# h of an agent-attention and SoLU kernel in 64-row tiles: three passes over both column halves, p turned two tiles at a time, its parts copied to both row halves by transfers

## The chip, the cores and the metric

The kernel runs on one core of one Trainium2 chip. A time is device microseconds (us) of one execution on that core; several executions give a median. One further execution was profiled, and every row below comes from that one.

## What is computed

Four batches of 12608 rows of q, k and v with 128 columns, and 49 agents per batch. The attention goes through the agents, and its result is the input x of a feed-forward block (50432 rows, 128 to 1024 and back), whose activation is a softmax-weighted h with a layer norm:

```python
a2k = sm(agents, k); agent_v = a2k @ v          # sm: softmax of scale * (a @ b.T)
q2a = sm(q, agents); x = q2a @ agent_v
h = x @ w_in
e = exp(h - max(h)); solu = h * e / sum(e)
ln = (solu - mean(solu)) / sqrt(var(solu) + 1e-06) * g_ln
out = ln @ w_out
```

All of it is float32.

## The kernel before, in words

The rows are handled in 396 tiles of 128 (99 a batch). For each batch, phase A (`phase_a`) makes agent_v in 13 chunks of k and v and multiplies it by w_in, so that h of a row is p times a matrix M with 49 rows and 1024 columns, where p is the row's softmax over the 49 agents. M is held as a high part `mh` and a low part `ml` (float32r, a float32 format that TensorE takes in one pass where float32 takes two), each written twice, into rows 0 to 63 and rows 64 to 127.

Phase B (`phase_b`, units of 8 tiles, each of two groups of four) makes p: `b0` the logits on TensorE (L647), `b1` to `b3r` the softmax, `b4` on GpSimd scales p (L676), rounds it to a high part (L678) and takes the rest as low part (L680), both into one 128-column row of `pack` (49 used columns from 0, 49 from 64), `b5` turns the four tiles on TensorE (L687), `b6` copies them out on ScalarE into `pT` (L692). A column of `pT` so has the high part of p in rows 0 to 63 and the low part in rows 64 to 127.

The rest goes tile by tile (x): `c_h` (L730) makes h in PSUM, for each half of 512 columns one matmul with `mh` and one with `ml`, all 128 rows deep, so that two passes give all four products of parts. Then the row maximum (DVE, L734), exp (ScalarE, L744), u = h*e (DVE, L749), the sum of squares (ScalarE, L755), eight transposes of u (`c_t`, L762), and the split of the turned u into parts: a half that is in `DIR` is split straight from PSUM (ScalarE L777, DVE L786), another is copied to SBUF (ScalarE, L781) and split by GpSimd (L790, L794). `c_w` (L810) multiplies by w_out, 24 matmuls of 256 columns for two tiles. GpSimd's small operations and a transfer through DRAM give the norm's factor (`rB`), and DVE's L875 applies it.

The order of the instructions on each engine is fixed ahead by `Plan`: each operation has an engine, a cost, a due time and those it depends on; the planner simulates the engines and takes among the startable ones the one with the earliest due time. The costs (such as 0.468 for one half of `c_h`) and the due offsets (the table of numbers `BD0` to `AEND`) are constants of the source. `kind` tells it the shape that a matmul uses the array in, and `SWITCH` what a change between kinds costs. An engine never leaves this order, and SyncE issues all transfers from one queue in the planned order too.

Of the kernel before, what the change touches and what calls it, by code (L numbers as in the profile page):

```python
# [9 lines left out]
F32 = mybir.dt.float32  # L10
F32R = mybir.dt.float32r
# [3 lines left out]
ALU = mybir.AluOpType  # L15
# [10 lines left out]
class Plan:  # L26
# [15 lines left out]
    def op(self, eng, fn, cost, due, deps=(), take=False, free=None, after=(), kind=1, shy=0.0):  # L42
        o = Op()
        o.kind, o.shy = kind, shy
        o.eng, o.fn, o.cost, o.due, o.take, o.free = eng, fn, cost, due, take, free
        o.deps, o.outs, o.end, o.bank = [d for d in deps if d is not None], [], None, None
        o.left = 0
        for d in o.deps + [d for d in after if d is not None]:
            if d.end is None:
                o.left += 1  # L50
                d.outs.append(o)
        if not o.left:
            self.push(o)
        return o
# [71 lines left out]
def kernel(  # L126
# [32 lines left out]
    BD0 = 13.69
    BD1 = 15.3  # L160
    BD2 = 9.96
    BD3 = -17.37
    BD4 = 0.17
    BD5 = 5.85
    DH = -3.24
    DMX = -8.66
    DEX = 0.61
    DU_ = -1.62
    DSQ = 20.92
    DT = -0.42  # L170
    DEV = -8.39
    DLD = 1.53
    DSP = -1.16
    DW = 3.3
    DR = 1.58
    DF_ = 5.14
# [12 lines left out]
    DMXL = 15.46  # L189
    DEXR = 5.1  # L190
    DEXL = -1.93
    DUR = -10.64
    DUL = -12.84
    DSQR = -10.36
    DSQL = -12.17
    DTR = -6.53
    DTL = -23.81
    DEVR = -0.65
    DEVL = 9.51
    DLDR = -16.59  # L200
    DLDL = 26.96
    DSPR = -6.09
    DSPL = 14.43
    DWR = 2.46
    DWL = -0.21
    RBL = 6.0
    ASTART = -3.67
    AEND = -2.04
    engs = (mybir.EngineType.PE, mybir.EngineType.Activation, mybir.EngineType.DVE, mybir.EngineType.Pool)
    SCALE = 1.0 / math.sqrt(C)  # L210
    INV = 1.0 / DF
# [422 lines left out]
    def phase_b(k, dues, gate=()):  # L634

        b, t0, nt = units_b[k]
        r = {}
        nq = (nt + GT - 1) // GT

        def b0(j0, j1, px=None):  # L640
            if px is not None:
                r["px"] = px
            qt, px = qts[k], r["px"]
            for j in range(j0, j1):
                for h in range(0, P, AP2):
                    o = col0(t0 + j) - col0(t0) + h
                    nc.tensor.matmul(px[h : h + AP2, j * A : (j + 1) * A], qt[:, o : o + AP2], ag_sb[:, b, :A],  # L647
                                     start=True, stop=True)
            r["lg"] = px[:, : nt * A].rearrange("p (t a) -> p t a", a=A)

        def b1():
            r["mx"] = tiny.tile([P, UB], F32, tag="mx", name=f"mx{b}_{t0}")
            nc.vector.tensor_reduce(out=r["mx"][:, :nt], in_=r["lg"], op=ALU.max, axis=AX.X)

        def b1s():
            mx, lg = r.pop("mx"), r.pop("lg")
            r["e"] = logits[k % 2][:, :nt, :]
            r["d"] = r["e"][:, :, :A]
            nc.vector.tensor_tensor(out=r["d"], in0=lg, in1=mx[:, :nt].unsqueeze(2).to_broadcast([P, nt, A]),
                                    op=ALU.subtract)  # L660

        def b2():
            nc.scalar.activation(out=r["d"], in_=r["d"], func=AF.Exp, scale=SCALE)

        def b3():
            r["s"] = tiny.tile([P, UB], F32, tag="sm", name=f"sm{b}_{t0}")[:, :nt]
            nc.vector.tensor_reduce(out=r["s"], in_=r["e"], op=ALU.add, axis=AX.X)

        def b3r():
            nc.vector.reciprocal(out=r["s"], in_=r["s"])  # L670

        def b4(q):
            m = min(GT, nt - q * GT)
            sl = slice(q * GT, q * GT + m)
            pk, dv = packs[q], r["d"][:, sl, :]
            nc.gpsimd.tensor_tensor(out=dv, in0=dv, in1=r["s"][:, sl].unsqueeze(2).to_broadcast([P, m, A]),  # L676
                                    op=ALU.mult)
            nc.gpsimd.tensor_scalar(out=pk[:, :m, :A].bitcast(F32R), in0=dv, scalar1=1.0, scalar2=0.0,  # L678
                                    op0=ALU.mult, op1=ALU.add)
            nc.gpsimd.tensor_tensor(out=pk[:, :m, AP2 : AP2 + A].bitcast(F32R), in0=dv, in1=pk[:, :m, :A],  # L680
                                    op=ALU.subtract)

        def b5(q, px):
            m = min(GT, nt - q * GT)
            r["pt", q] = px
            for j in range(m):
                nc.tensor.transpose(px[:, j * P : (j + 1) * P], packs[q][:, j, :], ident)  # L687

        def b6(q):
            m = min(GT, nt - q * GT)  # L690
            pT = pTs[b, t0 // GT + q] = bpool.tile([P, GT * P], F32R, tag="pT", bufs=PTB, name=f"pT{b}_{t0}_{q}")
            nc.scalar.copy(out=pT[:, : m * P], in_=r.pop(("pt", q))[:, : m * P])  # L692
# [12 lines left out]
        d2 = op("D", b1s, 0.05 + 0.0532 * nt, dues[1] + 0.1, [d1] + [B4.get((k - 2, q)) for q in range(2)], free=first, shy=shy)  # L705
        a1 = op("A", b2, 0.098 + 0.0402 * nt, dues[2], [d2])
        d3 = op("D", b3, 0.05 + 0.0532 * nt, dues[3], [a1], shy=shy)
        d5 = op("D", b3r, 0.12, dues[3] + 0.2, [d3])
        for q in range(nq):
            g = len(groups)  # L710
            groups.append((b, t0 // GT + q))
            sc = min(GT, nt - q * GT) / GT
            old = B5.get((k - 1, q)) or B5.get((k - 2, q))
            B4[k, q] = op("G", lambda q=q: b4(q), 0.07 + 1.5 * sc, dues[4] + 2.5 * q, [d5, old])
            B5[k, q] = op("P", lambda px, q=q: b5(q, px), 0.435 * sc, dues[5] + 2.5 * q,
                          [B4[k, q], grp_h.get(groups[g - PTB]) if g >= PTB else None], take=True, shy=shy)
            pT_op[groups[g]] = op("A", lambda q=q: b6(q), 0.48 * sc, dues[5] + 2.5 * q + 0.3, [B5[k, q]], free=B5[k, q], shy=shy)
# [5 lines left out]
    def c_h(x, hf):  # L723
        b, t = seq[x]
        g, j = divmod(t, GT)
        ph = phs[x] = ph2[x % 2]
        lhs = pTs[b, g][:, j * P : (j + 1) * P]
        sl = slice(hf * HW, (hf + 1) * HW)
        for m in range(2):
            nc.tensor.matmul(ph[:, sl], lhs, bmats[b]["mh" if m == 0 else "ml"][:, sl], start=(m == 0), stop=(m == 1))  # L730

    def c_max(x):
        nms[x] = tiny.tile([P, 1], F32, tag="nm", name=f"nm{x}")
# [159 lines left out]
    def F(f, *x):  # L893
        return lambda *y: f(*x, *y)
# [30 lines left out]
    def at(x, d, r, l):  # L925
        return x + d + (r * (1.0 - x / 12.0) if x < 12 else l if x >= (B - 1) * TB else 0.0)
# [4 lines left out]
    for x in range(n):  # L931
# [3 lines left out]
        if t % UB == 0:  # L935
# [7 lines left out]
        grp_h[b, t // GT] = last_h[b] = H[x, 1]  # L943
        MX[x] = op("D", F(c_max, x), 1.13, at(x, DMX, DMXR, DMXL), [H[x, 0], H[x, 1]])
# [116 lines left out]
```

## Time and profile before

| | |
|---|---|
| median of 3 executions | 1573.31 us (1573.09 to 1574.97) |
| the profiled execution | 1575.81 us, of which its span 1574.0 us |
| TensorE (PE) busy | 1550.8 us, 99% |
| ScalarE (ACT) busy | 1440.1 us, 91% |
| VectorE (DVE) busy | 1376.5 us, 87% |
| GpSimd (POOL) busy | 1254.5 us, 80% |
| granted TensorE clock, mean | 0.999 |

The span is from the first to the last instruction of the program. Busy is the time in which an engine has at least one instruction running. Matmuls overlap each other in the rows (one of 512 columns is shown with 0.39 us, and the next starts 0.23 us later), so what a matmul costs is read from one start to the next.

### The profile page before, as it was taken

To read this page: it belongs to the slowest core of one execution; us is meant where nothing else is said; L and a number is where in the kernel's file an instruction comes from. 1 tells how busy PE (TensorE), PEld (TensorE's weight loads), DVE (VectorE), ACT (ScalarE), POOL (GpSimd) and SP (SyncE) were. 2 spreads that over 40 slices of the span, in tenths; PEclk is the share of its full clock that TensorE was granted. 3 is DMA by queue.
4 is the path that set the end of the run, shared out by engine and by line. 5 is a ranking of instruction groups with operands and counts; after the bars stand their busy time and mean duration, and the time that the engine had idled before them with its cause. 6 is when DMAs were issued, how large, how long until landed. Compare 5 with 4: busy or idle time off the path is not lost.

```text
span 1574.0 us, 35069 instructions
## 1 busy us (share of the span) xinstructions
PE 1550.8 (99%) x12821; PEld 1381.7 (88%) x12821; DVE 1376.5 (87%) x2161; ACT 1440.1 (91%) x2740; POOL 1254.5 (80%) x1715
## 2 busy tenths in 40 slices
PE   8899999999999999999999999999999999999998
PEld 5588898998889899898899899898988989999998
DVE  6989898888998888889898888988888998989986
ACT  3599999999999999999999998999989999999996
POOL 2577888888788788787888878887878889988896
PEclk9999999999999999999999999999999999999999
DMA  9422323313123223222222232222111121111111
GB/s 370 150 88 81 96 81 95 95 59 103 62 82 100 82 88 105 91 81 74 88 68 88 88 102 88 88 88 87 49 63 53 47 69 55 62 55 49 45 42 40
DMA packets 57629, 133.65 MB, mean 85 GB/s; under 512 B 9840, under 2 KB 14064, under 8 KB 57456
## 3 DMA queue, kind: packets, MB, share of 16 engines
q1 hardware_dynamic: 57456, 131.41, 26.2%
q8 instruction: 101, 1.65, 0.4%
q14 instruction: 72, 0.59, 0.1%
HBM read 105.36 MB, written 26.02 MB: 83 GB/s over the span
## 4 chain that ended last, share of the span: by engine, by line
PE 89%; DVE 4%; ACT 3%; POOL 2%; issue 1%; DMA 0%; SPq 0%; DVEq 0%; ACTq 0%; POOLq 0%
PE px L810 33%; PE ph L730 22%; PE px L762 21%; PE px L647 3%; PE px L467 3%; PE px L418 3%; PE px L687 3%; PE px L451 1%; ACT e L744 1%; DVE u L749 1%; ACT sq L755 1%; DVE nm L734 1%; POOL uL L794 0%; ACT uT L781 0%; DVE mxp L423 0%
## 5 line engine op out<-in xcount | busy, mean ns | idle before, releaser
L794 POOL TENSOR_TENSOR uL<-uT,uH 128x1024 fp32r<-128x1024 f32 (+1 forms) x295 | 598.6, 2029 | 24.3
L734 DVE TENSOR_REDUCE nm<-ph 128x1 f32<-128x1024 f32 x396 | 480.3, 1219 | 55.3 <-PE ph L730 53.3
L749 DVE SCALAR_TENSOR_TENSOR u<-ph,e 128x1024 f32<-128x1024 f32 x396 | 481.0, 1219 | 54.2 <-ACT e L744 30.3
L755 ACT ACTIVATE sq<-u,su 128x1024 bf16<-128x1024 f32 x396 | 464.0, 1172 | 25.9 <-DVE u L749 22.8
L744 ACT ACTIVATE e<-ph,nm 128x1024 f32<-128x1024 f32 x396 | 446.3, 1132 | 28.4 <-DVE nm L734 25.0
L810 PE MATMUL px<-uL,wH 128*128 128x256 f32 x1584 | 467.2, 295 | 0.1
L810 PE MATMUL px<-uH,wH 128*128 128x256 f32 x1584 | 453.5, 286 | 2.6 <-DVE uL L786 1.4
L810 PE MATMUL px<-uH,wL 128*128 128x256 f32 x1584 | 449.4, 284 | 0.0
L762 PE MATMUL px<-ident,u 128*128 128x128 f32 x3168 | 429.4, 274 | 2.6 <-DVE u L749 0.7
L762 PEld LDWEIGHTS px<-ident,u 128*128 128x128 f32 x3168 | 355.6, 141 | 51.5 <-issue 18.7
L790 POOL TENSOR_SCALAR uH<-uT 128x1024 fp32r<-128x1024 f32 (+1 forms) x295 | 268.3, 909 | 85.7 <-ACT uT L781 84.6
L730 PE MATMUL ph<-mh,pT 128*128 128x512 f32 x792 | 326.3, 412 | 0.7 <-DVE u L749 0.4
L810 PEld LDWEIGHTS px<-uH,wH 128*128 128x128 f32 x1584 | 299.7, 189 | 15.4 <-issue 3.8
L730 PE MATMUL ph<-ml,pT 128*128 128x512 f32 x792 | 312.4, 394 | 0.0
L810 PEld LDWEIGHTS px<-uH,wL 128*128 128x128 f32 x1584 | 300.2, 189 | 9.6
L810 PEld LDWEIGHTS px<-uL,wH 128*128 128x128 f32 x1584 | 299.8, 189 | 9.0 <-issue 4.6
L781 ACT COPY uT<-px 128x512 f32<-128x512 f32 x492 | 272.9, 594 | 13.7 <-issue 3.0
L786 DVE TENSOR_TENSOR uL<-px,uH 128x512 fp32r<-128x512 f32 x300 | 200.9, 681 | 28.0 <-ACT uH L777 27.7
L777 ACT CAST uH<-px 128x512 fp32r<-128x512 f32 x300 | 170.1, 603 | 2.9 <-PE px L762 2.6
L730 PEld LDWEIGHTS ph<-mh,pT 128*128 128x128 f32 x792 | 149.2, 188 | 22.6 <-DVE u L749 4.6
L730 PEld LDWEIGHTS ph<-ml,pT 128*128 128x128 f32 x792 | 149.7, 189 | 17.1 <-DVE ml L543 0.2
L829 POOL TENSOR_TENSOR y<-x,nhalf 128x4 f32<-128x4 f32 x99 | 100.1, 1011 | 7.5
(119 smaller groups left out, 1469.2 us busy)
## 6 DMA issues: line engine op xcount, KB each, us to landing
rB<-dr SPq DMA_DIRECT2D x98, 256.0 KB
qt<-in_qT_dram SPq DMA_DIRECT2D x48, 512.0 KB
out_dram<-ob SPq DMA_DIRECT2D x95, 256.0 KB
kt<-in_kT_dram SPq DMA_DIRECT2D x36, 512.0 KB
vt<-in_v_dram SPq DMA_DIRECT2D x36, 512.0 KB
dr<-yr SPq DMA_DIRECT2D x392, 0.5 KB
kh<-in_kT_dram SPq DMA_DIRECT2D x12, 512.0 KB
vh<-in_v_dram SPq DMA_DIRECT2D x12, 512.0 KB
```

What stands on the lines that cost most here:

```text
L730: nc.tensor.matmul(ph[:, sl], lhs, bmats[b]["mh" if m == 0 else "ml"][:, sl], start=(m == 0), stop=(m == 1))
L734: nc.vector.tensor_reduce(out=nms[x], in_=phs[x], op=ALU.max, axis=AX.X, negate=True)
L744: nc.scalar.activation(out=es[x], in_=phs[x], func=AF.Exp, bias=nms.pop(x), accum_out=st[G]["S"][:, j : j + 1])
L749: nc.vector.scalar_tensor_tensor(out=u, in0=phs[x], scalar=INV, in1=es[x], op0=ALU.mult, op1=ALU.mult, accum_out=su)
L755: nc.scalar.activation(out=sq, in_=u, func=AF.Square, bias=su, scale=-float(DF), accum_out=st[G]["Q"][:, j : j + 1])
L762: nc.tensor.transpose(pt[:, kf * P : (kf + 1) * P], us[x][0][:, k0 * P : (k0 + 1) * P], ident)
L777: nc.scalar.copy(out=uH, in_=pt)
L781: nc.scalar.copy(out=rr[x][:, hf * 4 : hf * 4 + 4, :], in_=pt)
L786: nc.vector.tensor_tensor(out=uL, in0=pt, in1=uH.bitcast(F32), op=ALU.subtract)
L790: nc.gpsimd.tensor_scalar(out=uH, in0=rr[x][:, k0:k1, :], scalar1=1.0, scalar2=0.0, op0=ALU.mult, op1=ALU.add)
L794: nc.gpsimd.tensor_tensor(out=uL, in0=rr[x][:, k0:k1, :], in1=uH.bitcast(F32), op=ALU.subtract)
L810: nc.tensor.matmul(po, wt[:, kf, :], ut[:, kf, :], start=(q == 0), stop=(q == WM - 1))
```

## The change

`b4` only scales p now, into a `pack` of 64 columns a tile. `b5` turns two tiles with one transpose: rows 0 to 63 of the result belong to the even tile, rows 64 to 127 to the odd one. `b6` writes the high part from PSUM (half the columns of before), a new `b7` on DVE takes the low part from PSUM and the high part, and a new `b8` issues two transfers from SyncE for each group, which copy rows 0 to 63 to rows 64 to 127 of a second copy and the other way round. `c_h` makes both halves of 512 columns in one operation: six matmuls that are 64 rows deep, the left half in rows 0 to 63 of the array, the right half in rows 64 to 127, in three passes (high with `mh`, high with `ml`, low with `mh`; the product of the low parts is left out). The planner gets the cost 0.82 for all of `c_h` and kind 1 in place of 0. `DIR` is looked up by x % 8: five of sixteen halves go straight, where it was six. The due offsets are other numbers, and `pT` has 6 buffers of twice the size in place of 8.

```diff
-    DIR = {(1, 0), (1, 1), (3, 1)}
+    DIR = {(1, 0), (1, 1), (3, 1), (5, 1), (7, 1)}
...
-    BD4 = 0.17
-    BD5 = 5.85
+    BD4 = 8.39
+    BD5 = 8.87
...
-    PTB = 8
+    PTB = 6
...
-        pk = const.tile([P, GT, P], F32, name=f"pack{i}")
+        pk = const.tile([P, GT, AP2], F32, name=f"pack{i}")
...
-            nc.gpsimd.tensor_scalar(out=pk[:, :m, :A].bitcast(F32R), in0=dv, scalar1=1.0, scalar2=0.0,
-                                    op0=ALU.mult, op1=ALU.add)
-            nc.gpsimd.tensor_tensor(out=pk[:, :m, AP2 : AP2 + A].bitcast(F32R), in0=dv, in1=pk[:, :m, :A],
-                                    op=ALU.subtract)
+            nc.gpsimd.tensor_tensor(out=packs[q][:, :m, :A], in0=r["d"][:, sl, :],
+                                    in1=r["s"][:, sl].unsqueeze(2).to_broadcast([P, m, A]), op=ALU.mult)
...
-            for j in range(m):
-                nc.tensor.transpose(px[:, j * P : (j + 1) * P], packs[q][:, j, :], ident)
+            for j in range(0, m, 2):
+                nc.tensor.transpose(px[:, j * AP2 : (j + 2) * AP2], packs[q][:, j : j + 2, :].rearrange("p j a -> p (j a)"),
+                                    ident)
...
+            nc.scalar.copy(out=pT[:, 0, 0, :w], in_=r["pt", q][:, :w])
+
+        def b7(q):
...
+            nc.vector.tensor_tensor(out=pT[:, 0, 1, :w], in0=r.pop(("pt", q))[:, :w], in1=pT[:, 0, 0, :w].bitcast(F32),
+                                    op=ALU.subtract)
+
+        def b8(q):
...
+            for i in range(2):
+                r0, r1 = i * AP2, (1 - i) * AP2
+                nc.sync.dma_start(out=pT[r1 : r1 + AP2, 1, :, :w].bitcast(F32), in_=pT[r0 : r0 + AP2, 0, :, :w].bitcast(F32))
...
-        for m in range(2):
-            nc.tensor.matmul(ph[:, sl], lhs, bmats[b]["mh" if m == 0 else "ml"][:, sl], start=(m == 0), stop=(m == 1))
+        for q, (part, mm) in enumerate(((0, mh), (0, ml), (1, mh))):
+            for hf in range(2):
+                sl, rows = slice(hf * HW, (hf + 1) * HW), slice(hf * AP2, (hf + 1) * AP2)
+                nc.tensor.matmul(ph[:, sl], pTs[b, g][rows, (hf + j) % 2, part, tok], mm[rows, sl], start=(q == 0), stop=(q == 2))
...
-        for hf in range(2):
-            H[x, hf] = op("P", F(c_h, x, hf), 0.468, at(x, DH, DHR, DHL) + 0.02 * hf,
-                          [pT_op[b, t // GT], U.get(x - 2)] + mdone[b][: hf + 1], kind=0)
+        H[x] = op("P", F(c_h, x), 0.82, at(x, DH, DHR, DHL), [pT_op[b, t // GT], U.get(x - 2)] + mdone[b], kind=1)
```

Three places of the instruction order show what is moved.

PE in the second batch, before: transposes of u (L762), then h of one tile (L730, h in `ph`, p in `pT`) and c_w (L810) right behind it.

```order
L762 MATMUL px_127<-ident,u_9468 128x128 x4
L762 MATMUL px_125<-ident,u_9468 128x128 x4
L810 MATMUL px_124<-uL_9277,wH 128x256
L810 MATMUL px_124<-uH_9276,wL 128x256
L810 MATMUL px_124<-uH_9276,wH 128x256
L810 MATMUL px_124<-uL_9277,wH 128x256
L730 MATMUL ph_122<-mh_5775,pT_64_0_9358 128x512
L730 MATMUL ph_122<-ml_5776,pT_64_0_9358 128x512
L730 MATMUL ph_122<-mh_5775,pT_64_0_9358 128x512
L730 MATMUL ph_122<-ml_5776,pT_64_0_9358 128x512
L810 MATMUL px_124<-uH_9276,wL 128x256
```

PE in the second batch of the change: h is L743 now, transposes of u are L775, c_w is L823, and L467 is phase A's product with v, in tiles of 64 columns.

```order
L823 MATMUL px_126<-uH_9497,wL 128x256
L823 MATMUL px_126<-uH_9497,wH 128x256
L823 MATMUL px_126<-uL_9498,wH 128x256
L467 MATMUL px_124<-vt_9_9080,eT_9_9745 64x128 x8
L743 MATMUL ph_123<-mh_5727,pT_64_0_9520 128x512 x2
L743 MATMUL ph_123<-ml_5728,pT_64_0_9520 128x512 x2
L743 MATMUL ph_123<-mh_5727,pT_64_0_9520 128x512 x2
L775 MATMUL px_125<-ident,u_9715 128x128 x4
L823 MATMUL px_126<-uH_9497,wL 128x256
```

Six matmuls stand where four stood, in pairs on one part of M, and here a tile of phase A is directly ahead of them.

SP's queue in the third batch of the change: L701 are the new transfers, L864 and L865 send the norm's factor, L904 an output, L396 and L407 load k and v.

```order
L864 DMA dr_11971<-yr_11961 4x32 x4
L865 DMA rB_11972<-dr_11971 128x512
L701 DMA pT_8_0_12008<-pT_8_0_12008 64x512 x2
L396 DMA kt_2_12093<-in_kT_dram 128x1024
L904 DMA out_dram<-ob_12108 128x512
L396 DMA kt_3_12131<-in_kT_dram 128x1024
L407 DMA vt_2_12196<-in_v_dram 128x1024
L864 DMA dr_12209<-yr_12204 4x32 x4
L701 DMA pT_8_1_12222<-pT_8_1_12222 64x512 x2
```

Two transfers a group stand between those that were there before, and none of the others is gone.

## Rows read from the trace of the kernel before

**Rows 1.** The page, busy time: engine busy us (share of the span) xinstructions.

```profile
PE 1550.8 (99%) x12821; PEld 1381.7 (88%) x12821; DVE 1376.5 (87%) x2161; ACT 1440.1 (91%) x2740; POOL 1254.5 (80%) x1715
```

**Rows 2.** Windows: stretch, us, busy of PE PEld DVE ACT POOL (instructions), granted clock, DMA.

```profile
0.00:100.00 100.00, 85.24 (x726) 58.69 (x727) 79.14 (x153) 53.49 (x118) 46.04 (x68) 0.98 0.62 223
200.00:600.00 400.00, 398.92 (x3330) 357.34 (x3329) 353.21 (x554) 373.65 (x711) 322.03 (x442) 1.00 0.28 86
1200.00:1500.00 300.00, 298.31 (x2476) 276.64 (x2475) 273.24 (x410) 294.59 (x548) 261.87 (x363) 1.00 0.17 55
```

**Rows 3.** Timeline of PE, one c_h: start us, us, engine, line, out<-in, rows*columns, count.

```profile
810.03 0.40 PE L730 MATMUL ph<-mh,pT 128*128 128x512 f32 x1
...
810.95 0.28 PE L810 MATMUL px<-uH,wL 128*128 128x256 f32 x1
```

**Rows 4.** Timeline of PE around the logits of one unit (L647) and two sets of transposes.

```profile
816.08 0.28 PE L810 MATMUL px<-uH,wL 128*128 128x256 f32 x1
816.19 0.28 PE L810 MATMUL px<-uH,wH 128*128 128x256 f32 x1
816.40 1.14 PE L647 MATMUL px<-ag_sb,qt 128*64 128x49 f32 x32
817.47 0.66 PE L687 MATMUL px<-ident,pack 128*128 128x128 f32 x4
817.96 0.60 PE L762 MATMUL px<-ident,u 128*128 128x128 f32 x4
818.32 0.37 PE L810 MATMUL px<-uL,wH 128*128 128x256 f32 x1
818.52 0.28 PE L810 MATMUL px<-uH,wL 128*128 128x256 f32 x1
```

**Rows 5.** Lines by shape, PE, 480 to 760 us: xcount | busy us, mean ns | idle.

```profile
L810 PE MATMUL px<-uL,wH 128*128 128x256 f32 x290 | 87.2, 301 | 0.0
...
L730 PE MATMUL ph<-mh,pT 128*128 128x512 f32 x144 | 58.0, 403 | 0.0
```

**Rows 6.** Timeline of PE, one chunk of phase A (L418): two tiles of 64 columns.

```profile
219.84 1.08 PE L418 MATMUL px<-kt,ag_sb 128*64 128x512 f32 x4
220.85 1.09 PE L762 MATMUL px<-ident,u 128*128 128x128 f32 x8
```

**Rows 7.** Timeline of PE, one float32 matmul of 512 columns on the full array (L531).

```profile
807.82 1.02 PE L531 MATMUL px<-win_sb,av_dup 128*128 128x512 f32 x2
808.68 0.49 PE L762 MATMUL px<-ident,u 128*128 128x128 f32 x3
```

**Rows 8.** Timeline of PE around a matmul one row deep (L491).

```profile
401.10 0.28 PE L810 MATMUL px<-uH,wL 128*128 128x256 f32 x1
401.31 0.38 PE L491 MATMUL px<-ones,row 1*128 1x1 f32 x2
401.62 0.38 PE L810 MATMUL px<-uH,wH 128*128 128x256 f32 x1
401.84 0.29 PE L810 MATMUL px<-uL,wH 128*128 128x256 f32 x1
```

**Rows 9.** Timelines of PE in narrow windows: L467 turning to a tile 64 rows deep.

```profile
397.06 0.27 PE L467 MATMUL px<-vt,eT 128*64 128x128 f32 x1
...
397.26 0.32 PE L467 MATMUL px<-vt,eT 64*64 64x128 f32 x1
```

**Rows 10.** Timeline of PE, one whole L467 of phase A: 16 matmuls in eight pairs.

```profile
235.70 1.06 PE L467 MATMUL px<-vt,eT 128*64 128x128 f32 x16
236.69 0.44 PE L762 MATMUL px<-ident,u 128*128 128x128 f32 x2
```

**Rows 11.** Lines by shape, ACT: the copy of the turned p.

```profile
L692 ACT CAST pT<-px 128x512 fp32r<-128x512 f32 x96 | 57.7, 601 | 6.0 <-PE px L687 5.8
```

**Rows 12.** Waits of SP's queue: line, waited for, us in total, times, longest us.

```profile
SPq L891 <- DVE ob L875: 459.5, 83, 13.2
...
SPq L852 <- DMA dr<-yr: 53.3, 91, 2.6
```

More of the change, by code (lines that the diff above doesn't have):

```diff
@@ L157 @@
     WC = 4
[L159 to L162, printed above, removed]
-    BD4 = 0.17
-    BD5 = 5.85
[L165 to L176, printed above, removed]
+    BD0 = 11.79
+    BD1 = 12.29
+    BD2 = 10.71
+    BD3 = -17.5
+    BD4 = 8.39
+    BD5 = 8.87
+    DH = -6.46
+    DMX = 0.4
+    DEX = 5.54
+    DU_ = -2.31
+    DSQ = 29.74
+    DT = 0.31
+    DEV = -3.94
+    DLD = 3.07
+    DSP = -17.22
+    DW = 4.65
+    DR = 0.16
+    DF_ = 4.4
     OUTD = -5.86
@@ L188 @@
     DMXR = 10.02
[L189 to L192, printed above, removed]
+    DMXL = 10.71
+    DEXR = -5.26
+    DEXL = -3.36
+    DUR = -9.16
     DUL = -12.84
-    DSQR = -10.36
+    DSQR = -10.39
     DSQL = -12.17
[L196 to L199, printed above, removed]
+    DTR = -6.2
+    DTL = -20.21
+    DEVR = -8.06
+    DEVL = 9.39
     DLDR = -16.59
-    DLDL = 26.96
+    DLDL = 6.55
     DSPR = -6.09
-    DSPL = 14.43
-    DWR = 2.46
+    DSPL = 16.8
+    DWR = 2.63
     DWL = -0.21
     RBL = 6.0
-    ASTART = -3.67
-    AEND = -2.04
+    ASTART = -4.07
+    AEND = 1.37
     engs = (mybir.EngineType.PE, mybir.EngineType.Activation, mybir.EngineType.DVE, mybir.EngineType.Pool)
@@ L685, in b5 @@
             r["pt", q] = px
-            for j in range(m):
-                nc.tensor.transpose(px[:, j * P : (j + 1) * P], packs[q][:, j, :], ident)
+            for j in range(0, m, 2):
+                nc.tensor.transpose(px[:, j * AP2 : (j + 2) * AP2], packs[q][:, j : j + 2, :].rearrange("p j a -> p (j a)"),
+                                    ident)
         def b6(q):
-            m = min(GT, nt - q * GT)
-            pT = pTs[b, t0 // GT + q] = bpool.tile([P, GT * P], F32R, tag="pT", bufs=PTB, name=f"pT{b}_{t0}_{q}")
-            nc.scalar.copy(out=pT[:, : m * P], in_=r.pop(("pt", q))[:, : m * P])
+            w = (min(GT, nt - q * GT) + 1) // 2 * P
+            pT = pTs[b, t0 // GT + q] = bpool.tile([P, 2, 2, GT // 2 * P], F32R, tag="pT", bufs=PTB, name=f"pT{b}_{t0}_{q}")
+            nc.scalar.copy(out=pT[:, 0, 0, :w], in_=r["pt", q][:, :w])
+        def b7(q):
+            w = (min(GT, nt - q * GT) + 1) // 2 * P
+            pT = pTs[b, t0 // GT + q]
+            nc.vector.tensor_tensor(out=pT[:, 0, 1, :w], in0=r.pop(("pt", q))[:, :w], in1=pT[:, 0, 0, :w].bitcast(F32),
+                                    op=ALU.subtract)
+        def b8(q):
+            w = (min(GT, nt - q * GT) + 1) // 2 * P
+            pT = pTs[b, t0 // GT + q]
+            for i in range(2):
+                r0, r1 = i * AP2, (1 - i) * AP2
+                nc.sync.dma_start(out=pT[r1 : r1 + AP2, 1, :, :w].bitcast(F32), in_=pT[r0 : r0 + AP2, 0, :, :w].bitcast(F32))
         shy = SHY if k < 4 else 0.0
@@ L713, in phase_b @@
             old = B5.get((k - 1, q)) or B5.get((k - 2, q))
-            B4[k, q] = op("G", lambda q=q: b4(q), 0.07 + 1.5 * sc, dues[4] + 2.5 * q, [d5, old])
-            B5[k, q] = op("P", lambda px, q=q: b5(q, px), 0.435 * sc, dues[5] + 2.5 * q,
+            B4[k, q] = op("G", lambda q=q: b4(q), 0.08 + 0.53 * sc, dues[4] + 2.5 * q, [d5, old])
+            B5[k, q] = op("P", lambda px, q=q: b5(q, px), 0.218, dues[5] + 2.5 * q,
                           [B4[k, q], grp_h.get(groups[g - PTB]) if g >= PTB else None], take=True, shy=shy)
-            pT_op[groups[g]] = op("A", lambda q=q: b6(q), 0.48 * sc, dues[5] + 2.5 * q + 0.3, [B5[k, q]], free=B5[k, q], shy=shy)
+            a6 = op("A", lambda q=q: b6(q), 0.25, dues[5] + 2.5 * q + 0.3, [B5[k, q]], shy=shy)
+            d7 = op("D", lambda q=q: b7(q), 0.33, dues[5] + 2.5 * q + 0.6, [a6], free=B5[k, q], shy=shy)
+            pT_op[groups[g]] = op("S", lambda q=q: b8(q), (0.12, 0.13 if k else 0, 2.5), dues[5] + 2.5 * q + 0.6, [d7], shy=shy)
         if k + 2 < nu and k + 2 > 1:
@@ L721, with c_h @@
     us, phs, nms, es, rr, pr, st = {}, {}, {}, {}, {}, {}, {}
-    def c_h(x, hf):
+    def c_h(x):
         b, t = seq[x]
@@ L726, in c_h @@
         ph = phs[x] = ph2[x % 2]
-        lhs = pTs[b, g][:, j * P : (j + 1) * P]
-        sl = slice(hf * HW, (hf + 1) * HW)
-        for m in range(2):
-            nc.tensor.matmul(ph[:, sl], lhs, bmats[b]["mh" if m == 0 else "ml"][:, sl], start=(m == 0), stop=(m == 1))
+        mh, ml = (bmats[b][m] for m in ("mh", "ml"))
+        tok = slice(j // 2 * P, j // 2 * P + P)
+        for q, (part, mm) in enumerate(((0, mh), (0, ml), (1, mh))):
+            for hf in range(2):
+                sl, rows = slice(hf * HW, (hf + 1) * HW), slice(hf * AP2, (hf + 1) * AP2)
+                nc.tensor.matmul(ph[:, sl], pTs[b, g][rows, (hf + j) % 2, part, tok], mm[rows, sl], start=(q == 0), stop=(q == 2))
     def c_max(x):
@@ L764, in direct @@
     def direct(x, hf):
-        return (x % GT, hf) in DIR or x >= n - TD
+        return (x % (2 * GT), hf) in DIR or x >= n - TD
     def parts(x, k0, k1):
@@ L939 @@
             ku += 1
-        for hf in range(2):
-            H[x, hf] = op("P", F(c_h, x, hf), 0.468, at(x, DH, DHR, DHL) + 0.02 * hf,
-                          [pT_op[b, t // GT], U.get(x - 2)] + mdone[b][: hf + 1], kind=0)
-        grp_h[b, t // GT] = last_h[b] = H[x, 1]
-        MX[x] = op("D", F(c_max, x), 1.13, at(x, DMX, DMXR, DMXL), [H[x, 0], H[x, 1]])
+        H[x] = op("P", F(c_h, x), 0.82, at(x, DH, DHR, DHL), [pT_op[b, t // GT], U.get(x - 2)] + mdone[b], kind=1)
+        grp_h[b, t // GT] = last_h[b] = H[x]
+        MX[x] = op("D", F(c_max, x), 1.13, at(x, DMX, DMXR, DMXL), [H[x]])
         EX[x] = op("A", F(c_exp, x), 1.11, at(x, DEX, DEXR, DEXL), [MX[x], U.get(x - 2), RB.get(G - 3)] + (cout if x < 2 else []))
```

3 lines of the change are left out of this document (removed).

## The prediction

> **What bounds the kernel now.** First the busy times [rows 1]: PE has 99% of the span, ACT 91%, DVE 87%, POOL 80%. A busy PE need not be a full PE, since a matmul's row lasts longer than its place in the stream, so the windows come next [rows 2]. From 200 to 600 us PE is busy in 398.9 of 400 us and ACT in 373.7. From 1200 to 1500 us, where phase A is over, PE has 298.3 and ACT 294.6 of 300 us: there ACT is close behind. In the first 100 us PE waits for loads and is busy in 85 us.
>
> Then I test whether those PE rows are work or waiting, by giving each matmul the distance from its start to the next start. A pass of h takes 0.23 us, since four take 0.92 [rows 3]. A c_w matmul takes 0.11 to 0.12, four transposes 0.36, and the c_w matmul behind them lasts 0.20 in place of 0.12, so a transpose takes (0.36 + 0.08) / 4 = 0.11 [rows 4]. From 480 to 760 us there are 869 c_w matmuls (290 of one kind [rows 5]), 288 passes of h (144 of one kind [rows 5]), 695 transposes, and 30 runs of narrow matmuls at 1.1 to 1.2 us: 101 + 66 + 76 + 35 = 278 of 280 us. PE hardly waits. The time of the kernel is the sum of what PE is given, and a microsecond more or less on PE is one on the span, until ACT takes over.
>
> **The price that decides: a change of the array's shape.** All big matmuls of before use the full array, 128 rows by 128 columns. Phase A and the logits use tiles of 64 columns, two side by side. Reader, look at the two borders of such a run. Ahead of L647 the last c_w matmul lasts 0.21 us (816.19 to 816.40) where the one before it lasted 0.11: 0.10 us in which nothing streams [rows 4]. L418 has four matmuls of 512 columns in 1.01 us [rows 6], and one such product, two matmuls on the full array, takes 0.86 [rows 7]. So the two tiles do run side by side (else it were 1.72), and 0.15 us are left for leaving the shape and for the first load of weights. The row depth counts as well as the width: going to a matmul one row deep costs 0.21 - 0.12 = 0.09 [rows 8], and L467 going from 128 rows to 64 rows takes 0.20 [rows 9] where its own steps take (0.99 - 0.10) / 8 = 0.11 [rows 10]: again 0.09. I take 0.095 for each change.
>
> Behind a change the first weights are loaded in the open, since the load cannot run ahead of it: the first c_w matmul after L491 takes 0.22 in place of 0.12, so 0.10 [rows 8]; the first transposes after L647 take 0.49 in place of 0.44, so 0.05 [rows 4]; a 64-column tile is left with 0.15 - 0.095 = 0.055 [rows 6, 7].
>
> The Trainium skill ("TensorEngine Tiling (Array Packing)", Key Properties) says that changing the tiling mode drains the engine, and names no price. No run here shows 64 rows by 128 columns, which is the shape of the new h; by that rule it pays like the others.
>
> **The change part by part.**
>
> 1. *h itself.* Four passes of 0.23 become three, if the two row tiles run side by side as the column tiles do [rows 6, 7], and 0.01 for the second tile's later start: 0.92 - 0.70 = 0.22, times 396 tiles = **-87.1 us**. Bounds: three passes at the array's float32 rate of half of 0.43 (0.215) save 18 us more; not side by side is a rival.
>
> 2. *Changes of shape.* Counted over the whole PE order, the shape changes 277 times before and 983 times now: 380 runs of the new h (14 of the 396 follow another h directly) are entered and left, though 53 of them come straight from a column tile and 15 go straight to one. 706 x 0.095 = **+67.1 us**.
>
> 3. *First loads.* The new h loads 128 columns, as c_w does, so I take 0.10 for it and not the 0.055 of a 64-column tile: 380 x 0.10 = **+38.0**. If both tiles load one after the other it is 0.20. Behind a tile shape now stand 152 more c_w (or float32) matmuls at 0.10, **+15.2**, 166 more transposes at 0.05, **+8.3**, and 8 more column tiles, +0.4.
>
> 4. *Turning p.* 200 transposes in place of 396: 196 x 0.11 = **-21.6**.
>
> Sum on PE: -87.1 + 67.1 + 38.0 + 15.2 + 8.3 + 0.4 - 21.6 = **+20.3 us**.
>
> 5. *Beside PE.* ACT's copy of p has 256 columns in place of 512: 0.60 us [rows 11] falls to something between half and all of it, so at most 30 us of 1440 go, all under PE. POOL loses two of its three operations on p and gains one half-tile split per 8 tiles; DVE loses that split and gains b7. Both had 10% or more to spare in every long window [rows 2], and PE, longer now, covers them. I cost them at nothing. If PE were shorter, ACT would bind next.
>
> 6. *The transfers.* h of a group now needs `b8`: the second matmul of c_h waits for the landing, and all of PE stands behind it, because it keeps its order. Worked out with the steps above, the transposes of p stand 9 to 38 us of PE work ahead of their first h (10 to 18 in the last batch). Between them lie two short operations, the issue, and a landing; SP waited at most 2.6 us for landing of the small `dr` transfers [rows 12]. SP itself waits most of its time for DVE (459.5 us in 83 waits [rows 12]), so 200 more issues fit; the copies queue behind those waits, the longest 13.2 us. Cost taken: nothing, with a rival below. Six buffers of `pT` hold 24 tiles, about 95 us: no wait.
>
> Against the profiled span: 1574.0 + 20.3 = 1594.3; that execution's own time, 1575.8, stands 2.5 above the median of the runs shown, 1573.3. I give the median of the change: 1573.3 + 20.3 = **1594 us**, slower by 1.3%. A measurement of this kernel tells about 0.2% (3 us) from no change.
>
> **Rivals.**
>
> *A change of shape costs h little (faster).* The planner's new cost for all of c_h is 0.82, which is 0.70 and 0.12 for both borders together. Then PE gives back 0.10 x 396 + 21.6 = 61 us: 1512. With no price at all it would be 87.1 + 21.6 = 109, 1465; ACT with its 1440 - 30, and the 46 us of the first 100 in which it has nothing to do [rows 1, 2], would stop that at about 1460 as well. It decides as soon as both borders together cost less than 0.27 us (0.22 + 21.6/396). For it: no row has this very shape. Against it: every border seen, between three kinds of shapes, shows 0.09 to 0.10 [rows 4, 8, 9]. Chance 0.20. The Trainium skill ("TensorEngine Tiling (Array Packing)", Theoretical Speedup) promises up to twofold for products of 64 rows or fewer; by that alone the time would be this rival's lower end.
>
> *Each pass loads its weights in the open (slower).* Then the second and third pass pay 0.10 too: 2 x 0.10 x 396 = 79, 1673. Against it: the steps of L467, each with new weights, are 0.11, the same as a full-array transpose that loads [rows 4, 10], so its loads are hidden. The Trainium skill ("TensorE: Matmul & The Clock Gate", Part 3, The mechanism) lets loads overlap running matmuls only where the row group differs. With both row groups busy that would give this rival; rows 10 speak against it. Chance 0.06.
>
> *The row tiles run one after the other.* Six passes: 3 x 0.23 x 396 = 273 us more, about 1867. Against it the column tiles [rows 6, 7]. Chance 0.03.
>
> *PE waits for the copies.* If SP is held as long as its longest wait, 13.2 us [rows 12], a group with 9 us of lead is late by some 4 us and the landing. One group in ten late by 4 us: 40 us, 1634. Chance 0.05.
>
> My forecast has the rest, 0.66; its own range is 1573 (first load of the new h at 0.055) to 1632 (both tiles load in turn).
>
> **How the numbers follow.** Faster: the first rival's 0.20 and 0.02 from the lower end of the forecast, 0.22. Within 0.2%: 0.06, also from there. Slower: 0.72. The range goes down to the first rival's upper value and up to the forecast's end with part of the late copies: 1512 to 1632. It leaves out the cheaper half of the first rival (0.10), the loads (0.06) and the serial tiles (0.03).
>
> **What would show it.** In the profile of the change: the start of the new h some 0.2 us after the matmul ahead of it starts a c_w step of 0.12; its pairs start within 0.01 us of each other; three passes 0.23 apart, the first 0.33 long; 0.09 to 0.10 us of nothing behind the last, and a c_w of 0.22 after it; about 1.07 us a tile in all. PE stays at 98 to 99% busy with ACT falling to under 90%. No long wait of PE for a transfer of `pT`. If the matmul ahead of h keeps its 0.12 and the one behind starts at once, the prices of steps 2 and 3 were wrong and the time lies near 1465 to 1512; if the pairs start 0.23 apart, step 1 was.

## The result, and the profile after

The change takes 1578.72 us (median of 10 runs), the kernel before, on the same chip, 1574.38 us (10 runs). The ratio is 1.0027, with a 95% interval of 1.0017 to 1.0037. So it is slower, by 4.3 us, where 20.3 were forecast; the range (1512 to 1632) holds it. One of the ten runs took 3696.45 us, alone among all runs of this study; the ratio leaves it out, and without it the median is 1578.43. The profiled execution has a span of 1577.3 us at a mean granted clock of 0.999, against 1574.0 before.

The page of the change, busy times and, from the part on the chain that ended last, the shares by engine:

```profile
PE 1558.1 (99%) x13415; PEld 1269.5 (80%) x13415; DVE 1380.8 (88%) x2221; ACT 1427.7 (91%) x2731; POOL 1254.5 (80%) x1613
...
PE 96%; DVE 2%; ACT 0%; DMA 0%; issue 0%; SPq 0%; ACTq 0%; DVEq 0%
```

Beside [rows 1]: PE is busy 7 us longer, ACT 12 us less, POOL as long as before. The second line had no counterpart among the rows read before the prediction, and it should have had one. On the page of the kernel before it reads:

```profile
PE 89%; DVE 4%; ACT 3%; POOL 2%; issue 1%; DMA 0%; SPq 0%; DVEq 0%; ACTq 0%; POOLq 0%
```

Before, 11% of the chain stood on something else than PE; now it is 4%. The table behind the experiments shows how far that share can be trusted. The windows of the change, against [rows 2] (same columns):

```profile
200.00:600.00 400.00, 399.57 (x3444) 324.46 (x3444) 352.88 (x563) 370.83 (x709) 321.22 (x412) 1.00 0.34 102
1200.00:1500.00 300.00, 299.83 (x2619) 252.77 (x2620) 272.60 (x418) 291.31 (x550) 268.26 (x341) 1.00 0.26 76
```

PE's idle time is down from 1.1 to 0.4 us in the middle and from 1.7 to 0.2 at the end. In the first 100 us PE is busy in 84.9, against 85.2.

**The new h** in the timeline of PE of the change (start, us, engine, line, out<-in, rows*columns, count), once between c_w and transposes of u and once between two sets of transposes:

```profile
1296.32 0.28 PE L823 MATMUL px<-uL,wH 128*128 128x256 f32 x1
1296.44 0.28 PE L823 MATMUL px<-uH,wL 128*128 128x256 f32 x1
1296.64 0.50 PE L743 MATMUL ph<-mh,pT 64*128 64x512 f32 x2
1296.98 0.40 PE L743 MATMUL ph<-ml,pT 64*128 64x512 f32 x2
1297.21 0.40 PE L743 MATMUL ph<-mh,pT 64*128 64x512 f32 x2
1297.55 0.66 PE L775 MATMUL px<-ident,u 128*128 128x128 f32 x4
1298.13 0.50 PE L743 MATMUL ph<-mh,pT 64*128 64x512 f32 x2
```

Read it by starts, against [rows 3]. The last c_w matmul holds the stream for 0.20 us (1296.44 to 1296.64) where the one ahead held it 0.12: a border of 0.09 (unrounded, 0.206 is usual ahead of h and 0.117 between two c_w). The first pass lasts 0.34, the second 0.23, the third 0.34, which is 0.23 and a border of 0.10. The pair of the second pass stands in one row of 0.40 us, no longer than a single matmul of h before [rows 3]: the two row tiles run side by side (in the records behind the row their starts are 3 to 4 ns apart). Four transposes then take 0.58 us, of which 0.44 are the transposes, 0.09 the next border and 0.05 the first load. Every price of the forecast is there.

**PE's work, one price list for both kernels.** I priced every matmul of both orders alike (change of shape 0.094, first load 0.05 to 0.10, pass of h 0.232 or 0.2335 for a pair, transpose 0.109, c_w 0.1166) from h of tile 8 to h of tile 390. Between the two kernels the shape changes add 64.6 us and the loads 62.6, h gives 86.9 and the turning of p 20.2: **+20.1 us**, against the 20.3 forecast for the whole kernel. What is left of the elapsed time above the priced work is booked as waiting:

| tile 8 to 390 | elapsed | priced | waits |
|---|---|---|---|
| before | 1436.4 | 1419.7 | 16.7 |
| change | 1450.0 | 1446.6 | 3.5 |

(Of the 26.9 by which the priced work differs, 6.8 are c_w and transposes that lie outside this stretch in the kernel before.) The waits fall by 13.2 us; before and behind the stretch the change is 10.4 us shorter, 3.6 of them more than the 6.8 that moved. 20.1 - 13.2 - 3.6 = 3.3, the difference of the two spans. So PE's work grew as forecast, and 17 us went elsewhere: 13.2 of waits, and 3.6 at the ends that nothing here traces (the way to h of tile 8 takes 96.31 us in the trace before and 93.95 in that of the same kernel with more PE work below, so some of it may be chance).

The waits can be counted a second way, without a price list: a matmul counts as late if it starts over 15 ns later than the median, over all twelve traces, for its shape between the same neighbours. By place, as this is called below, the stretch has 13.0 us of waits before and 1.9 in the change. So 11 of the 13.2 us are starts that came late; the other 2 are small differences in the spacing of matmuls, which a single price books as waiting. Of the 13.0 us, 0.8 lie between 480 and 760 us, 3.6 between 800 and 1200, and 5.7 behind 1200; in the change 0.3 lie there.

**A wait that a busy engine hides.** In the last stage of the kernel before, each unit of 28 us has this place; PE, then DVE, then the weight loads (PEld):

```profile
1333.58 1.04 PE L762 MATMUL px<-ident,u 128*128 128x128 f32 x8
1334.65 0.50 PE L730 MATMUL ph<-mh,pT 128*128 128x512 f32 x1
1334.99 0.39 PE L730 MATMUL ph<-ml,pT 128*128 128x512 f32 x1
```

```profile
1333.38 1.22 DVE L749 SCALAR_TENSOR_TENSOR u<-ph,e 128x1024 f32<-128x1024 f32 x1
```

```profile
1334.65 0.19 PEld L730 LDWEIGHTS ph<-mh,pT 128*128 128x128 f32 x1 [0.27 <-DVE u L749]
```

Eight transposes hold the stream for 0.88 us, so h could start at 1334.46. It starts at 1334.65, right behind the end of DVE's u (1334.60), which frees `ph`. PE's row of the transposes lasts to 1334.62, so the profile counts 0.03 us of idle time, and the wait was 0.19. It also costs the first load, which starts together with the pass: that one takes 0.34 in place of 0.23. That is 0.30 us lost, a tenth of it shown in PE's row; the row of the weight loads shows 0.27. The chain doesn't show it either: there it runs through PE, with 0.04 us of issue. Ten such places from 1278 to 1530 us make some 3 of the 13.0 us; the others are spread over many kinds.

### The profile page after: what moved, and what is told of

Read it like the earlier page. It is cut to its first block, busy times and chain, and to the rows that moved or that the text cites. A ratio compares the mean times of both kernels' runs of the same rounds, so it can differ in the third digit from the quotient of the medians.

```text
span 1577.3 us, 36659 instructions
## 1 busy us (share of the span) xinstructions
PE 1558.1 (99%) x13415; PEld 1269.5 (80%) x13415; DVE 1380.8 (88%) x2221; ACT 1427.7 (91%) x2731; POOL 1254.5 (80%) x1613
## 4 chain that ended last, share of the span: by engine, by line
PE 96%; DVE 2%; ACT 0%; DMA 0%; issue 0%; SPq 0%; ACTq 0%; DVEq 0%
PE px L823 37%; PE px L775 24%; PE ph L743 22%; PE px L647 3%; PE px L418 3%; PE px L467 3%; PE px L682 2%; PE px L451 1%; PE px L531 0%; DVE mxp L423 0%; DMA kh<-in_kT_dram 0%; DVE nm L747 0%; DVE ca_in L263 0%; DVE u L762 0%; ACT ek L444 0%
## 5 line engine op out<-in xcount | busy, mean ns | idle before, releaser
L807 POOL TENSOR_TENSOR uL<-uT,uH 128x1024 fp32r<-128x1024 f32 (+1 forms) x344 | 660.5, 1920 | 28.7
L762 DVE SCALAR_TENSOR_TENSOR u<-ph,e 128x1024 f32<-128x1024 f32 x396 | 479.7, 1219 | 67.2 <-ACT e L757 44.3
L823 PE MATMUL px<-uH,wH 128*128 128x256 f32 x1584 | 470.1, 297 | 0.4 <-DVE ob L888 0.3
L823 PE MATMUL px<-uH,wL 128*128 128x256 f32 x1584 | 467.0, 295 | 0.0
L775 PE MATMUL px<-ident,u 128*128 128x128 f32 x3168 | 463.1, 277 | 0.2 <-ACT uT L794 0.2
L823 PE MATMUL px<-uL,wH 128*128 128x256 f32 x1584 | 454.9, 287 | 0.0
L803 POOL TENSOR_SCALAR uH<-uT 128x1024 fp32r<-128x1024 f32 (+1 forms) x344 | 298.2, 867 | 156.4 <-ACT uT L794 149.5
L775 PEld LDWEIGHTS px<-ident,u 128*128 128x128 f32 x3168 | 351.5, 141 | 85.5 <-issue 46.0
L743 PE MATMUL ph<-mh,pT 64*128 64x512 f32 x1584 | 350.9, 442 | 4.0 <-DVE u L762 4.0
L794 ACT COPY uT<-px 128x512 f32<-128x512 f32 x541 | 311.0, 591 | 44.4 <-PE px L775 24.6
L823 PEld LDWEIGHTS px<-uH,wH 128*128 128x128 f32 x1584 | 299.8, 189 | 21.7 <-issue 17.9
L823 PEld LDWEIGHTS px<-uL,wH 128*128 128x128 f32 x1584 | 299.2, 189 | 21.1 <-issue 21.0
L823 PEld LDWEIGHTS px<-uH,wL 128*128 128x128 f32 x1584 | 298.8, 189 | 20.7 <-issue 20.5
L743 PEld LDWEIGHTS ph<-mh,pT 64*128 64x128 f32 x1584 | 148.7, 184 | 88.0 <-issue 23.4
L799 DVE TENSOR_TENSOR uL<-px,uH 128x512 fp32r<-128x512 f32 x251 | 169.6, 681 | 6.1 <-ACT uH L790 5.7
L790 ACT CAST uH<-px 128x512 fp32r<-128x512 f32 x251 | 148.7, 599 | 12.9 <-PE px L775 12.1
L743 PE MATMUL ph<-ml,pT 64*128 64x512 f32 x792 | 157.7, 394 | 0.0
L757 ACT ACTIVATION_READ_ACCUMULATOR e<-ph,nm 128x1 f32 x396 | 82.9, 209 | 0.0
```

The lines of the kernel that those rows point to most:

```text
L743: nc.tensor.matmul(ph[:, sl], pTs[b, g][rows, (hf + j) % 2, part, tok], mm[rows, sl], start=(q == 0), stop=(q == 2))
L757: nc.scalar.activation(out=es[x], in_=phs[x], func=AF.Exp, bias=nms.pop(x), accum_out=st[G]["S"][:, j : j + 1])
L762: nc.vector.scalar_tensor_tensor(out=u, in0=phs[x], scalar=INV, in1=es[x], op0=ALU.mult, op1=ALU.mult, accum_out=su)
L790: nc.scalar.copy(out=uH, in_=pt)
L794: nc.scalar.copy(out=rr[x][:, hf * 4 : hf * 4 + 4, :], in_=pt)
L799: nc.vector.tensor_tensor(out=uL, in0=pt, in1=uH.bitcast(F32), op=ALU.subtract)
```

## The experiments

Two theories for the missing 17 us. **A:** the kernel before had small waits of PE for other engines, and a longer PE fills them. **B:** the new due offsets and `DIR` make a better order, whatever PE's work is. Later a third, **C:** ACT's shorter copy of p took the waits away. Of every kernel the profile's chain is read, and the waits as above.

**More work on PE, in both kernels.** One transpose of u is issued twice in every second tile, 198 more of 0.109 us.

```diff
-            nc.tensor.transpose(pt[:, kf * P : (kf + 1) * P], us[x][0][:, k0 * P : (k0 + 1) * P], ident)
+            for _ in range(2 if x % 2 == 0 and hf == 0 and kf == 0 else 1):
+                nc.tensor.transpose(pt[:, kf * P : (kf + 1) * P], us[x][0][:, k0 * P : (k0 + 1) * P], ident)
```

In the kernel before:

> The kernel before, with one transpose of u issued twice in every second tile: 198 more transposes of 0.109 us, 21.6 us more work for PE, same result, same order otherwise. Theory A (PE before had some 17 us of small waits, and a longer PE fills them): the time grows by clearly less than the work, by 5 to 13 us. Theory B (PE before was full; the change won its time back by its other order and its other DIR): it grows by 20 to 22 us.

In the change:

> The changed kernel with the same 198 transposes issued twice, 21.6 us more work for PE. Theory A: PE of the changed kernel has few waits left (some 4 us between tile 8 and tile 390), so the time grows by 17 to 22 us over the changed kernel's 1578.7. Theory B says the same, so this is the measure for the run beside it: under A the kernel before grows by much less than this one, under B by the same.

Measured: 1591.25 us from before (ratio 1.0105, 1.0091 to 1.0119), +16.8 of 21.6; 1599.48 us from the change (ratio to before 1.0157, 1.0144 to 1.0171), +20.8 of 21.6. In the kernel before the waits fall from 16.7 to 12.0 us; in the change they stay (3.5 and 3.0). So a microsecond on PE is one on the span in the change and not in the kernel before: there 4.8 us went into waits. Of the expectations for the kernel before, neither holds: 16.8 (14.3 to 18.7 by the interval) lies between the 5 to 13 of A and the 20 to 22 of B. What A names is there, but it gives only some 5 of the 17.

**The offsets and DIR, exchanged.** The kernel before with the change's numbers, and the change with those of before; here three of the numbers:

```diff
-    DIR = {(1, 0), (1, 1), (3, 1)}
+    DIR = {(1, 0), (1, 1), (3, 1), (5, 1), (7, 1)}
...
-    DH = -3.24
+    DH = -6.46
...
-    DSP = -1.16
+    DSP = -17.22
```

> The kernel before with the due offsets and the DIR of the change, and nothing else of it: h, the turning of p and the buffers as before. Theory A: the order is worth little, the time is within 4 us of before. Theory B: the order is what gave the time back, so it is faster than before by 10 to 17 us.

> The changed kernel with the due offsets and the DIR of before. Theory A: within 5 us of the changed kernel. Theory B: slower than it by 10 to 17 us, at 1589 to 1596, where the sum of the prediction had put the change.

Measured: both are slower. Before with the new numbers 1595.57 us (1.0128, 1.0111 to 1.0145), 21 more; the change with the old ones 1606.33 us (1.0203, 1.0189 to 1.0217), 27.6 more than with its own. The chain of before with the new numbers:

```profile
PE 70%; POOL 19%; DVE 4%; ACT 3%; issue 3%; DMA 2%; SPq 0%; POOLq 0%; DVEq 0%; ACTq 0%
```

POOL still does its three operations on p there and gets one half-tile split more per 8 tiles: it is busy 1347.0 us in place of 1254.5, and the chain runs over it for 19%. The waits are 26.3 us there and 25.1 in the change with old numbers, where the waits of PE show one kind that the change itself has none of, h held by the copies of p:

```profile
PE ph L743 <- DMA pT<-pT: 1.7, 2, 1.1
```

None of the four forecasts held (within 4 or 5 us under A; 10 to 17 faster and 10 to 17 slower under B). B falls as it was put: the numbers by themselves don't help. Each kernel is over 20 us slower with the numbers of the other.

**Only DIR back.** The change with its own offsets and the `DIR` of before (looked up by x % 4).

```diff
-    DIR = {(1, 0), (1, 1), (3, 1), (5, 1), (7, 1)}
+    DIR = {(1, 0), (1, 1), (3, 1)}
...
-        return (x % (2 * GT), hf) in DIR or x >= n - TD
+        return (x % GT, hf) in DIR or x >= n - TD
```

> The changed kernel with its own due offsets but the DIR set of before (six of sixteen halves straight from PSUM, looked up by x % 4): one half-tile in sixteen more is split by DVE and ACT and one less by GpSimd. If the loss of 27.6 us with the old offsets and the old DIR came from the offsets, this costs less than 5 us: below 1584. If it came from DIR, the time is near 1600 or above. In between means that both count, and that offsets and DIR are fitted to each other.

Measured: 1591.66 us (1.0108, 1.0091 to 1.0125), 13 more than the change, with waits of 18.0. In between: about half of the 27.6 goes with `DIR`. POOL falls to 1164.8 us of busy time, and DVE, which gets that half-tile, rises from 1380.8 to 1405.5. The waits of PE for DVE's u grow; the change, then this run:

```profile
PE ph L743 <- DVE u L762: 4.0, 4, 2.4
...
PE ph L743 <- DVE u L762: 6.9, 12, 2.4
```

Offsets made for the other set may have a part in it, but they are not all: a pair of full-depth kernels below differs in `DIR` alone, with the offsets of before, and there too the old `DIR` is slower.

**More work on ACT.** In the change, `b6` copies 128 columns once more, so that what the change took from ACT is given back.

```diff
             nc.scalar.copy(out=pT[:, 0, 0, :w], in_=r["pt", q][:, :w])
+            nc.scalar.copy(out=pT[:, 0, 0, :P], in_=r["pt", q][:, :P])
```

> The changed kernel, with a second ScalarE copy of 128 columns in b6 for each group (the same values are written again right after), about 0.28 us each, 100 groups: some 28 us more work on ScalarE, which is what the change took from it; the planned order stays. If the small waits of TensorE before the change were owed to ScalarE's load (its relief is what paid for the 11 us that are still unexplained), the time goes up by 8 us or more, to 1587 or above. If it was the order fitted to the new costs together with the longer TensorE, ScalarE has slack and the time stays within 3 us of 1578.7.

Measured: 1580.3 us (1.0036, 1.0023 to 1.0049), 1.6 more than the change. The copies, lines by shape of that kernel on ACT:

```profile
L688 ACT CAST pT<-px 128x256 fp32r<-128x256 f32 x100 | 38.4, 384 | 10.6 <-PE px L682 10.0
L689 ACT CAST pT<-px 128x128 fp32r<-128x128 f32 x100 | 26.6, 266 | 3.2
```

26.6 us more on ACT, which is more than the 22 that the shorter copies had saved (0.60 [rows 11] to 0.38 us, 100 times), and the time hardly moves. C falls for the order of the change; ACT's load was not varied in the kernel before.

**The change without its shapes.** The two-tile turning, the split from PSUM, the new `b7` and the offsets stay; four transfers a group, each 64 rows, put high and low part of a tile under one another, and h is made in four full-depth passes again. The planner still believes 0.82 and kind 1, so that the order stays the change's.

```diff
-            for i in range(2):
-                r0, r1 = i * AP2, (1 - i) * AP2
-                nc.sync.dma_start(out=pT[r1 : r1 + AP2, 1, :, :w].bitcast(F32), in_=pT[r0 : r0 + AP2, 0, :, :w].bitcast(F32))
+            lo, hi = slice(0, AP2), slice(AP2, P)
+            for dst, ds, src, ss in ((lo, 2, lo, 0), (hi, 2, lo, 1), (hi, 3, hi, 0), (lo, 3, hi, 1)):
+                nc.sync.dma_start(out=pT[dst, ds, :w].bitcast(F32), in_=pT[src, ss, :w].bitcast(F32))
...
-        for q, (part, mm) in enumerate(((0, mh), (0, ml), (1, mh))):
-            for hf in range(2):
-                sl, rows = slice(hf * HW, (hf + 1) * HW), slice(hf * AP2, (hf + 1) * AP2)
-                nc.tensor.matmul(ph[:, sl], pTs[b, g][rows, (hf + j) % 2, part, tok], mm[rows, sl], start=(q == 0), stop=(q == 2))
+        for hf in range(2):
+            sl = slice(hf * HW, (hf + 1) * HW)
+            for q, mm in enumerate((mh, ml)):
+                nc.tensor.matmul(ph[:, sl], pTs[b, g][:, 2 + j % 2, tok], mm[:, sl], start=(q == 0), stop=(q == 1))
```

> The changed kernel with h on the full array again: p is turned two tiles at a time and split from PSUM as in the change, but four transfers of 64 rows put high and low part of a tile above each other, so that h is four passes 128 rows deep as before. The planner keeps its cost of 0.82, so the order is that of the change. Shape theory (the prediction's prices: shape changes and first loads 129 us, third-pass saving 87 us): PE loses 42 us of work against the change, and the time falls to 1537 to 1550, 1537 where no new waits come. If the shapes were cheap and the change's time came from elsewhere, it rises towards 1640, since h itself is 87 us longer.

Measured: **1547.27 us**, ratio to before 0.9836 (0.9821 to 0.9851). It beats both kernels, by 27 and by 31 us. h and the c_w ahead of it in its timeline of PE:

```profile
804.06 0.28 PE L823 MATMUL px<-uH,wL 128*128 128x256 f32 x1
804.18 0.28 PE L823 MATMUL px<-uH,wH 128*128 128x256 f32 x1
804.30 0.39 PE L743 MATMUL ph<-mh,pT 128*128 128x512 f32 x1
804.53 0.40 PE L743 MATMUL ph<-ml,pT 128*128 128x512 f32 x1
```

No border: the c_w matmul keeps its 0.12, the first pass its 0.23. The priced work of the stretch is 1412.5 us, 34.1 less than the change's (42 was expected, and the forecast of the time holds), and the waits are 7.3, 3.8 more; -34.1 + 3.8 = -30.3, and 31.4 were measured. With 7.2 us less priced work in the stretch than the kernel before it also waits 9.4 us less, and that is not A, by which a shorter PE waits longer. From 1200 to 1500 us ACT is busy in 297.7 of its 300 us, close to the bound.

**The same kernel in other orders.** Three versions of it. First with the true cost of h told to the planner (0.936 and kind 0):

```diff
-        H[x] = op("P", F(c_h, x), 0.82, at(x, DH, DHR, DHL), [pT_op[b, t // GT], U.get(x - 2)] + mdone[b], kind=1)
+        H[x] = op("P", F(c_h, x), 0.936, at(x, DH, DHR, DHL), [pT_op[b, t // GT], U.get(x - 2)] + mdone[b], kind=0)
```

> As the run before it, with the planner told the measured cost of h on the full array, 0.936, and no change of shape. Work on PE is the same, so the time differs only by how the order fits: 1537 to 1560 under the shape theory.

Then with the offsets of before (all but `BD4` and `BD5`, which belong to the new p), and with its `DIR` too:

> As the run before it, with the due offsets of the kernel before (but the early turning of p kept) and the DIR of the change. Work on PE is 21.6 us less than before the change. If offsets are fitted to one set of costs, this sits between: 1553 plus 0 to 20 us of waits.

> As the run before it, with the DIR of before as well, six of sixteen halves straight from PSUM, which leaves GpSimd some 6% less work and VectorE some 3% more. Fitted-offsets theory: 1553 plus 0 to 20 us of waits, and below the run before it if GpSimd was what PE waited for.

Measured: 1558.96 us (0.9908, 0.9893 to 0.9923), 1556.95 us (0.9895, 0.9880 to 0.9909) and 1562.6 us (0.9929, 0.9913 to 0.9946). The instructions of the first two are those of the full-depth kernel above, and the order alone costs 11.7 and 9.7 us. A truer cost for the planner made it worse; that the offsets had been fitted with 0.82 would explain it, but no run shows how they were found. The last two differ in `DIR` alone: the old one costs 5.7 us more, although it leaves POOL less work, so POOL was not what PE waited for. The last one has the offsets and `DIR` of before and all of the change's handling of p: 18.6 us less priced work on PE than before, of which 11.8 arrive; its waits are 26.3 us, and its chain has PE at 81%. So b6, b7 and b8 don't remove the waits by themselves; the offsets and `DIR` that came with them do.

Waits in tiles 8 to 390, by the price list and by place:

| kernel | us | priced | by place | PE's share of the chain |
|---|---|---|---|---|
| before | 1574.4 | 16.7 | 13.0 | 89% |
| before, more PE work | 1591.3 | 12.0 | 9.4 | 90% |
| before, new offsets and DIR | 1595.6 | 26.3 | 25.6 | 70% |
| change | 1578.7 | 3.5 | 1.9 | 96% |
| change, more PE work | 1599.5 | 3.0 | 1.8 | 96% |
| change, old offsets and DIR | 1606.3 | 25.1 | 24.4 | 92% |
| change, old DIR | 1591.7 | 18.0 | 14.2 | 89% |
| change, more ACT work | 1580.3 | - | 4.2 | 95% |
| full depth, order of the change | 1547.3 | 7.3 | 6.5 | 91% |
| full depth, true cost | 1559.0 | 18.3 | 15.8 | 84% |
| full depth, old offsets | 1557.0 | - | 15.1 | 83% |
| full depth, old offsets and DIR | 1562.6 | 26.3 | 23.6 | 81% |

The two counts rank the kernels alike but for the three largest; a dash was not priced. The chain's share doesn't follow them: 92% stands beside 25.1 us, and 89% beside 16.7.

## Why the prediction was right and wrong

*The shape price, steps 1 to 3: right.* Three passes of 0.23, 0.01 more for the pair, 0.09 a border, 0.10 for the first load of h, 0.05 for transposes behind it, all as forecast, though no row had a tile of 64 rows by 128 columns. The Trainium skill ("TensorEngine Tiling (Array Packing)", Key Properties) has the engine drained at each change of mode; the trace now agrees for this mode too, with 0.09 us. The full-depth kernel confirms the sum from the other side: without the borders the c_w matmul ahead of h keeps 0.12, and 31.4 us come back.

*Step 4, turning p: right*, -20.2 in the stretch for -21.6 in the whole kernel.

*The step that failed* is the one in "What bounds the kernel now": "PE hardly waits", and with it "a microsecond more or less on PE is one on the span". It was drawn from one stretch, 480 to 760 us, by a sum of 278 of 280 us. The sum is made of rounded steps (0.11 to 0.12 a c_w matmul: over 869 of them the rounding alone is 9 us), which can't tell waits of 1% from none. And the stretch happens to be a good one: by place it has 0.8 us of waits in 280, while 5.7 of the 13.0 us lie behind 1200 us, where only the busy share was read. The kernel before waited 16.7 us, about 1.2%. Measured by itself, 21.6 us more on PE cost 16.8 there. PE's work grew by 20.1; the waits fell by 13.2 and the ends by 3.6.

*What the forecast left out* is the order and `DIR`. Its sum has no term for the other due offsets, and in step 5 it put the half-tile that DVE and ACT give to POOL at nothing ("I cost them at nothing"). The experiments show that offsets, `DIR` and work that don't belong together cost 10 to 28 us, more than the whole difference in question. Some 5 of the 17 us are a longer PE filling waits (the doubled transposes). `DIR` is the largest piece that a run isolates: the change with the old one takes 1591.7 us, 13 more and close to the forecast; with the offsets of before, at full depth, it is 5.7. The pieces overlap and don't add up. That the order alone can make waits of this size is shown by the full-depth kernels: same instructions, waits of 7.3 or 18.3 us. That it made the change's gain, beside `DIR` and the longer PE, is argued by exclusion: ACT's relief is worth 1.6 us, and the new handling of p has 26.3 us of waits with the old offsets and `DIR`. Whether the old kernel, with its offsets fitted afresh to its own costs or with the new `DIR` alone, would also lose its 16.7 us was not tried, so how much of the gain belongs to the change and how much to a better fit stays open.

*Step 5: right for ACT, wrong for `DIR`.* ACT's copy fell from 0.60 to 0.38 us, and giving ACT 26.6 us back cost 1.6. ACT stays at 91%, not under 90%, since the kernel came out shorter than forecast. POOL and DVE lengthened nothing, but moving the half-tile was a gain, of 6 to 13 us with the new handling of p.

*Step 6: right.* SP's waits for DVE's ob are fewer (459.5 [rows 12] to 281.4 us), and the transfers queue behind DVE themselves (the longest wait of the queue before was not the 13.2 us of the rival but 15.3, of a load of k that waits for PE); the waits of the change's SP queue:

```profile
SPq L904 <- DVE ob L888: 281.4, 63, 10.7
...
SPq L701 <- DVE pT L693: 184.8, 65, 8.4
```

PE waited for none of the copies. With the old offsets it did, twice, for 1.7 us.

*The rivals.* The cheap shape change falls: its borders cost 0.19, and with the first load of h (0.10) and of what follows (0.05 to 0.10) more than the 0.27 from which it decided. Loads in the open in every pass fall: the second and the third start 0.23 us after the one before, and the third has new weights in both row groups. A list in the Trainium skill ("TensorE: Matmul & The Clock Gate", Part 3, The mechanism), by which a load overlaps only where the row group differs, and the trace disagree: this load is hidden behind a pass in the same rows, which fits the opening of that section, where a load into the background weight buffer goes ahead too. Serial row tiles and late copies fall too. The rival that would have held was missing: a PE that is 99% busy and still waits.

*The chances.* 0.06 for "within 0.2%" and 0.72 for slower: the time came out at +0.27%, on the edge between the two, for which the forecast's own range (from 1573) had room only by a cheaper load, not by the waits. Its lower end is also off by its own terms: a first load of 0.055 saves 380 x 0.045 = 17 us, which gives 1577. That the range holds the time is luck.

## What to carry to other kernels

Before calling an engine full, measure its waits from start to start, over the whole kernel and not in one stretch: a TensorE 99% busy had 17 us of waits, which its overlapping rows hid, and work added to it was paid only in part. Its share of the chain is a hint and no measure of them. Where an order is fitted by numbers, compare two variants only when both are fitted, or keep the order and change one thing; here the same instructions differed by 10 to 12 us by the order alone, and by 28 with `DIR`. Going to half-depth tiles saved a quarter of the passes and gave it back in borders (0.19 us) and loads (0.10 to 0.20 us) around each 0.70 us of work; stacking the parts in the rows kept the gain of the cheaper turning without them.

## What was not expected

- A wait of PE for an operand costs more than the wait: the load of the next weights isn't hidden behind it (0.34 in place of 0.23 for the first pass of h).
- A truer cost in the planner made the kernel 11.7 us slower. That the due offsets had been fitted to the untrue one is the likely reason, and was not shown.
